# One order for the whole attention-and-mixer kernel, found by list scheduling, in place of a hand-written interleaving

## The chip, the cores and the metric

The kernel runs on one core of a Trainium2 chip. The metric is device time in microseconds (us) of one launch, from DRAM inputs to the DRAM output. The engines are named as in the profile: PE (matrix multiply), PEld (its weight loads), DVE (vector), ACT (scalar), POOL (GpSimd) and SP (here only a queue that issues transfers). Each engine works through its own instructions strictly in the order in which the program emitted them and waits on semaphores where it needs another engine's result.

## The reference, cut to what matters

```python
# q, k, v: 4 batches x 8 heads x 768 x 64; sort_net: 4 x 8 x 8 x 8
P = sort_net
for _ in range(5):                       # 5 Sinkhorn steps on each 8 x 8 matrix
    P = exp(P - max(P, -1)); P = P / (sum(P, -1) + 1e-9); P = P / (sum(P, -2) + 1e-9)
k_sorted, v_sorted = einsum("bhij,bhjcd->bhicd", P, k_blocks), same for v   # 8 blocks of 96 rows
scores = q_b @ k_sorted_b.T / 8          # per block: 96 x 96
x = softmax(scores) @ v_sorted_b         # then heads side by side: x is 4 x 768 x 512
wq, wk = x @ w_q, x @ w_k                # 512 -> 64
mixed = (wq @ wk.T / 8) @ x              # 768 tokens with 768 tokens
out = relu(mixed) @ w_out                # 512 -> 512, float32
```

The maximum that the reference takes off in its softmax cancels, and the kernel leaves it out there. Of the mixer, the kernel forms wk.T @ x (64 x 512) first, and then wq times that.

## The kernel before, in words

Work goes by batch b (4) and block i (8 blocks of 96 tokens). In the text a **unit** is a run of matmuls into one PSUM buffer together with the copy ("eviction") that empties it. The kinds, with the lines of their matmuls and evictions:

- Q (L162; L166 and L167): the queries of two heads, transposed, 12 transposes; two copies into the zero-padded QZ. Four units a batch.
- K (L186; L190): mixes the 8 key blocks by P (through the matrix M) and transposes, 12 matmuls; four units a batch, into KT.
- V (L206; L209): the same for values, 2 matmuls; four units, into VS. Then eight transfers on SP's queue (T, L215) turn VS into VT, one per block.
- S (L228; L235): scores of one block, 4 matmuls; ACT takes the exponential into E. Eight a batch.
- AV (L243; L249 and L250): E times VT with the row sums as a 65th column, 8 matmuls; DVE divides into X. Eight a batch.
- XT (L258; L262): X of two blocks transposed. Four a batch.
- The mixer `moe(b)`: WQ (L270; L275), WK (L281; L284), A (L289; L293), four MIX (L303; L310 on DVE, L312 on ACT) and three OUT units (L320; L326 on ACT, one L324 on DVE), each OUT followed by a transfer of 512 KB to DRAM (L327).

PSUM has three buffers of two banks (`ps`, used by K, V, S, AV, WQ, MIX, OUT) and two of one bank (`ps1`: Q, XT, WK, A). A unit waits until the buffer that it takes in turn has been emptied.

POOL issues the loads: q, k and v of each batch, 768 KB each as they land, in the order Q0 K0 V0 Q1 K1, the three weights, V1 Q2 K2 V2 Q3 K3 V3, with its memsets and the making of M (L173) among them.

What sets the order: the prologue is written out; then a loop goes over the 32 blocks `(b, i)` and emits S one block ahead, AV, and after every second block XT. Between them it emits pieces of a queue `Work`, in equal shares of estimated cost up to block 7: first the Q, K and V units of batch b+1, and from i = 1 on the mixer of batch b-1, strictly one generator after the other. The engine of each eviction is written at the call. The mixer of the last batch runs alone after the loop (`drain(moe(B - 1))`).

Of the kernel before, what the change touches and what calls it, by code (L numbers as in the profile page):

```python
# [17 lines left out]
def kernel(
# [133 lines left out]
    Xb = {}  # L152
    XT = {}
    KT = {}
    VT = {}
    Ms = {}

    def q_unit(b, kp, eng):
# [95 lines left out]
    def xt(b, i0):  # L254
        ps = psum1([P, PT, 2 * BLK], BF16)
        for ii in range(2):
            for pt in range(PT):
# [4 lines left out]
        nc.vector.tensor_copy(XT[b][:, :, i0 * BLK:(i0 + 2) * BLK], ps)  # L262

    def moe(b):
        X, Xt = Xb[b], XT[b]
# [8 lines left out]
        wqT = rot.tile([P, S], BF16, tag="wqT", name="wqT")
        nc.scalar.copy(wqT.rearrange("p (a n) -> p a n", a=2), ps[:, :, 0:hf])  # L275
        yield 8 * 163
        ps = psum1([P, NB, DH])
        for i in range(NB):
            m = P if i < NB - 1 else BLK
            for pt in range(PT):  # L280
                nc.tensor.matmul(ps[0:m, i, :], Xt[:, pt, i * BLK:i * BLK + m], wk_t[:, pt, :],  # L281
                                 start=(pt == 0), stop=(pt == PT - 1), skip_group_check=True)
# [11 lines left out]
        yield 8 * 107
        mixT = rot.tile([P, PT, R6, P], BF16, tag="mixT", name="mixT")
        wqv = wqT.rearrange("p (i r s) -> p r i s", i=NB, r=R6)
        ni = NB // 2
        n = 0
        for p2 in range(2):
            for hh in range(2):  # L300
                ps = psum([P, 2, 512])
                for a in range(2):
                    nc.tensor.matmul(ps[:, a, 0:hf], Ab[a * DH:(a + 1) * DH, p2 * P:(p2 + 1) * P],  # L303
                                     wqv[a * DH:(a + 1) * DH, :, hh * ni:(hh + 1) * ni, :],
                                     start=True, stop=True, skip_group_check=True)
# [151 lines left out]
```

## Time and profile before

| what | value |
|---|---|
| median of 3 runs | 148.35 us (147.12 to 149.61) |
| the profiled execution | 149.07 us; its span, first to last instruction, 147.2 us |
| PE busy | 101.9 us (69%), 1277 matmuls recorded |
| DVE busy | 78.8 us (54%) |
| ACT busy | 72.2 us (49%) |
| mean granted TensorE clock | 0.928 |
| DMA | 19.77 MB, mean 134 GB/s |

How to read it: times are from the span's start. A row of the timeline gives start, length, engine, line, operation and tiles, and in brackets how long the engine stood idle just before and what released it. The length of a group of matmuls contains the last one's run to its end, so the next group can start before it is over. "PEclk" is the share of the full 2.4 GHz that was granted; 0.5 is the lower level, 1.2 GHz.

### The profile page before, as it was taken

What the parts mean: (1) busy time and instruction counts of PE and PEld (TensorE: products, weight loads), DVE (VectorE), ACT (ScalarE), POOL (GpSimd) and SP (SyncE); (2) the same over time, 40 slices, a digit from 0 to 9 for tenths busy, and PEclk for the clock granted to TensorE, in tenths of its full rate; (3) what the DMA queues carried; (4) which work ended last, traced back from release to release, by engine and by line L of the source; (5) the groups of instructions that cost most, each with busy time, mean ns of one, the idle gap of its engine ahead of it and who ended that gap; (6) DMA issues with size and microseconds to landing.
All of it is one profiled execution on the core that took longest, in us unless ns stands there. A gap on an engine that the chain in (4) does not pass through costs nothing.

```text
span 147.2 us, 3040 instructions
## 1 busy us (share of the span) xinstructions
PE 101.9 (69%) x1277; PEld 69.7 (47%) x1284; DVE 78.8 (54%) x171; ACT 72.2 (49%) x97; POOL 28.3 (19%) x31
## 2 busy tenths in 40 slices
PE   0041987349874987778877876788976995965960
PEld 0031946336653946444556473546852454641320
DVE  4876880797777645444489256335464237215030
ACT  4018269444760786636538847355572444213220
POOL 7997499930040000000000000000000000000000
PEclk9999999996999599999999999999997799685599
DMA  1999999999999999903420057035100154000055
GB/s 8 179 204 204 204 205 192 232 246 205 204 204 230 246 205 205 241 11 143 176 109 4 0 97 122 3 159 216 57 0 4 51 215 161 0 4 0 0 222 206
DMA packets 19437, 19.77 MB, mean 134 GB/s; under 512 B 2017, under 2 KB 17889, under 8 KB 19425
## 3 DMA queue, kind: packets, MB, share of 16 engines
q0 software_dynamic: 14064, 10.09, 45.4%
q1 hardware_dynamic: 5360, 9.50, 20.4%
q8 instruction: 10, 0.16, 0.4%
q14 instruction: 3, 0.02, 0.0%
HBM read 20.19 MB, written 6.29 MB: 180 GB/s over the span
## 4 chain that ended last, share of the span: by engine, by line
PE 39%; DVE 17%; DMA 16%; ACT 14%; issue 6%; POOL 6%; ACTq 0%; SPq 0%; DVEq 0%; POOLq 0%
PE ps L320 16%; DMA Vn<-in_v_dram 8%; DMA VT<-VS 7%; ACT ot L326 6%; DVE X L250 5%; DVE mixT L310 4%; PE ps L270 4%; ACT KT L190 4%; PE ps L281 3%; PE ps L243 3%; PE ps L289 3%; PE ps L228 3%; PE ps L258 2%; DVE wkb L284 2%; DVE XT L262 2%
## 5 line engine op out<-in xcount | busy, mean ns | idle before, releaser
L235 ACT ACTIVATE E<-ps 96x768 bf16<-96x768 f32 x32 | 25.3, 808 | 12.0 <-PE ps L228 11.9
L320 PE MATMUL ps<-wo_t,mixT 128*128 128x512 bf16 x89 | 25.8, 429 | 6.3 <-DVE mixT L310 3.7
L326 ACT COPY ot<-ps 128x1024 f32<-128x1024 f32 x11 | 11.1, 1012 | 23.9 <-PE ps L320 17.1
L250 DVE TENSOR_TENSOR X<-ps,R 96x512 bf16<-96x512 f32 x32 | 22.0, 686 | 1.1
L320 PEld LDWEIGHTS <-mixT 128*128 128x128 bf16 x96 | 9.9, 106 | 19.4 <-issue 7.4
L262 DVE COPY XT<-ps 128x768 bf16<-128x768 bf16 x16 | 8.9, 557 | 19.0 <-PE ps L258 18.8
L243 PE MATMUL ps<-VT,E 96*128 96x65 bf16 (+1 forms) x256 | 14.4, 199 | 5.2 <-DMA VT<-VS 3.8
L228 PE MATMUL ps<-QZ,KT 128*96 128x192 bf16 x128 | 15.9, 249 | 2.8 <-ACT E L235 1.7
L243 PEld LDWEIGHTS <-E 96*128 96x128 bf16 (+1 forms) x256 | 12.6, 104 | 8.9 <-issue 4.8
L190 ACT CAST KT<-ps 128x768 bf16<-128x768 f32 x15 | 11.1, 808 | 8.2 <-PE ps L186 8.2
L162 PE MATMUL ps<-idb,Qn 128*64 128x128 bf16 x192 | 8.8, 252 | 8.8 <-DMA Qn<-in_q_dram 8.7
L249 DVE RECIPROCAL R<-ps 96x8 f32<-96x8 f32 x32 | 6.3, 196 | 16.0 <-PE ps L243 16.0
L228 PEld LDWEIGHTS <-KT 128*96 128x96 bf16 x128 | 11.6, 125 | 3.7 <-issue 3.5
L258 PE MATMUL ps<-idb,X 96*128 96x96 bf16 x128 | 9.3, 212 | 5.7 <-DVE X L250 3.6
L162 PEld LDWEIGHTS <-Qn 128*64 128x64 bf16 x192 | 7.3, 130 | 9.7 <-DMA Qn<-in_q_dram 8.7
L258 PEld LDWEIGHTS <-X 96*128 96x128 bf16 x128 | 7.3, 101 | 9.3 <-DVE X L250 4.6
L166 DVE COPY QZ<-ps 64x768 bf16<-64x768 bf16 x14 | 7.7, 547 | 4.9 <-PE ps L162 4.7
L186 PE MATMUL ps<-M,Kn 128*64 128x128 bf16 x192 | 9.5, 270 | 0.7 <-DVE M L173 0.5
L209 ACT CAST VS<-ps 128x768 bf16<-128x768 f32 x11 | 8.5, 813 | 2.3 <-PE ps L206 2.3
L310 DVE TENSOR_SCALAR mixT<-ps 128x768 bf16<-128x768 f32 x8 | 7.5, 954 | 3.8 <-PE ps L303 3.8
L206 PE MATMUL ps<-Vn,M 128*128 128x384 bf16 x32 | 8.5, 377 | 1.2 <-ACT VS L209 0.6
L186 PEld LDWEIGHTS <-Kn 128*64 128x64 bf16 x192 | 8.5, 144 | 1.1 <-issue 1.0
(65 smaller groups left out, 114.7 us busy)
## 6 DMA issues: line engine op xcount, KB each, us to landing
out_dram<-ot SPq DMA_DIRECT2D x12, 512.0 KB, 2.6
VT<-VS SPq DMA_DIRECT2D x32, 97.5 KB, 5.3
Qn<-in_q_dram POOLq DMA_DIRECT2D x4, 768.0 KB, 19.0
Kn<-in_k_dram POOLq DMA_DIRECT2D x4, 768.0 KB, 20.8
Vn<-in_v_dram POOLq DMA_DIRECT2D x4, 768.0 KB, 23.1
wo_t<-in_moe_w_out_dram POOLq DMA_DIRECT2D x1, 512.0 KB, 17.3
wq_t<-in_moe_w_q_dram POOLq DMA_DIRECT2D x1, 64.0 KB, 15.3
wk_t<-in_moe_w_k_dram POOLq DMA_DIRECT2D x1, 64.0 KB, 15.0
```

Of the source, the lines that this page charges most:

```text
L162: nc.tensor.matmul(ps[hh * D:(hh + 1) * D, r, :], Qn[b][:, 2 * kp + hh, r, :], idb, is_transpose=True, start=True, stop=True, skip_group_c ...
L186: nc.tensor.matmul(ps[hh * D:(hh + 1) * D, r * P:(r + 1) * P], Kn[b][:, h, r, :], Ms[b][:, h].rearrange("p i s -> p (i s)"), start=True, s ...
L190: eng(KT[b][:, kp], ps[:, 0:S].rearrange("p (r s) -> p s r", r=R6))
L228: nc.tensor.matmul(ps[0:BLK, kp // 2, (kp % 2) * 2 * BLK:(kp % 2 + 1) * 2 * BLK], KT[b][:, kp, i * SP:(i + 1) * SP].rearrange("p s r -> p ...
L235: nc.scalar.activation(E.rearrange("p (a n) -> p a n", a=2), ps[0:BLK, :, 0:4 * BLK], ACT.Exp, scale=scale)
L243: nc.tensor.matmul(ps[0:m, h // 4, (h % 4) * D1:(h % 4 + 1) * D1], E[:, h * BLK:h * BLK + m], VT[b][:, i, h, :], start=True, stop=True, sk ...
L250: nc.vector.tensor_mul(Xb[b][:, i].rearrange("p (a t d) -> p a t d", a=2, t=4), pv[:, :, :, 0:D], Rt.unsqueeze(3).to_broadcast([BLK, 2, 4, ...
L258: nc.tensor.matmul(ps[:, pt, ii * BLK:(ii + 1) * BLK], Xb[b][:, i0 + ii, pt * P:(pt + 1) * P], idb[0:BLK, 0:BLK], is_transpose=True, start ...
L262: nc.vector.tensor_copy(XT[b][:, :, i0 * BLK:(i0 + 2) * BLK], ps)
L310: nc.vector.tensor_relu(ov, iv)
L320: nc.tensor.matmul(ps[:, rr, :], mixT[:, pt, r0 + rr, :], wo_t[:, pt, :], start=(pt == 0), stop=(pt == PT - 1), skip_group_check=True)
L326: nc.scalar.copy(ot, ps)
```

## The change

The prologue up to M and PTR stays. All later work is described as about 230 objects `Unit` (209 of them planned by the function below, transfers included) with a PE cost, the eviction's cost on each engine allowed, the units it depends on, the units that must have read a buffer before it is overwritten, and a due time from a table `DUE`. `plan` is a list scheduler: among units that its model says could start within 60 ns of the earliest, it takes the one due first, and gives its eviction to the engine that would end it first. The kernel then emits the units in that order. Numbers in the table and in `plan` set the order alone; nothing waits for a time.

Units change too. WQ and WK are two halves each, so that they need only half of XT. MIX is split by token residue rather than by block, so that the first OUT needs only two MIX units. The last batch's OUT is six units of one bank (`ps1`) with transfers of 256 KB. Q, K, V, XT, WQ, WK, A, MIX and OUT may be evicted by ACT or DVE. M has three buffers in place of two, and M of batch 2 is made before the loop. The doubled w_q comes by two loads in place of one load and an ACT copy (L400). Engine, number and size of the other instructions are as before: 2570 rows on PE in both.

```diff
--- before.py
+++ after.py
+SW, LPE, LEV, LSLOT, LDMA = 95, 245, 90, 60, 3500
+SLOTS = {"b": 3, "s": 2}
+FREE = {"PE": 14500, "ACT": 16300, "DVE": 15900, "DMA": 14500}
+LAND = {"Q": [9000, 24500, 35500, 46500], "K": [12500, 28300, 39300, 50300],
+        "V": [16300, 32000, 43000, 54000], "W": 28000}
+PERIOD = 18000
+DUE = {
+    "Q": [(-33441, 1952), (-29592, 640), (-21240, 1562), (-20283, 640)],
...
+}
+class Unit:
+    def __init__(self, key, pe, mode, tag, ev, deps=(), war=(), ready=0):
+        self.key, self.pe, self.mode, self.tag, self.ev = key, pe, mode, tag, ev
+        self.deps, self.war, self.ready = list(deps), list(war), ready
+        off, step = DUE[key[0]][key[1]]
+        self.due = key[1] * PERIOD + off + step * key[2]
+
+def all_units(B, NB, NP, R6):
+    us = []
+
+    def add(*a):
+        us.append(Unit(*a))
+
+    for b in range(B):
+        old = b >= 2
+        kps, hs = range(NP), range(2)
+        s_old = [("S", b - 2, i) for i in range(NB)] if old else []
+        av_old = [("AV", b - 2, i) for i in range(NB)] if old else []
+        mix_old = [("MIX", b - 2, n) for n in range(4)] if old else []
+        outs = [(r, 1) for r in range(R6)] if b == B - 1 else [(r, 2) for r in range(0, R6, 2)]
+        for kp in kps:
+            if b or kp >= 2:
+                add(("Q", b, kp), 320, "c", "s", {"DVE": 1130, "ACT": 1420}, [], s_old,
+                    LAND["Q"][b])
+            add(("K", b, kp), 320, "c", "b", {"ACT": 700, "DVE": 880}, [], s_old, LAND["K"][b])
+            add(("V", b, kp), 326, "f", "b", {"ACT": 700, "DVE": 880}, [], [], LAND["V"][b])
+        qk = [(c, b, kp) for kp in kps for c in "QK" if b or kp >= 2 or c == "K"]
+        for i in range(NB):
+            n = b * NB + i - 8
+            add(("T", b, i), 0, None, None, {"DMA": 600}, [("V", b, kp) for kp in kps], av_old)
+            add(("S", b, i), 332, "f", "b", {"ACT": 700}, qk,
+                [("AV", n // NB, n % NB)] if n >= 0 else [])
+            add(("AV", b, i), 232, "f", "b", {"DVE": 885}, [("S", b, i), ("T", b, i)],
+                [("A", b - 2, 0)] + [("XT", b - 2, j) for j in range(4)] if old else [])
+        for j in range(4):
+            add(("XT", b, j), 344, "f", "s", {"DVE": 474, "ACT": 620},
+                [("AV", b, 2 * j), ("AV", b, 2 * j + 1)],
+                [(c, b - 2, h) for c in ("WK", "WQ") for h in hs] if old else [])
+        for h in hs:
+            xts = [("XT", b, 2 * h), ("XT", b, 2 * h + 1)]
+            add(("WQ", b, h), 652, "f", "b", {"ACT": 420, "DVE": 480}, xts, mix_old, LAND["W"])
+            add(("WK", b, h), 496, "f", "s", {"DVE": 350, "ACT": 370}, xts,
+                [("A", b - 2, 0)] if old else [], LAND["W"])
+        add(("A", b, 0), 856, "c", "s", {"ACT": 330, "DVE": 350},
+            [("WK", b, h) for h in hs] + [("AV", b, i) for i in range(NB)], mix_old)
+        for n in range(4):
+            add(("MIX", b, n), 170, "r", "b", {"ACT": 700, "DVE": 870},
+                [("A", b, 0)] + [("WQ", b, h) for h in hs],
+                [("OUT", b - 2, r) for r in range(0, R6, 2)] if old else [])
+        for r, w in outs:
+            halves = sorted({r * 2 // R6, (r + w - 1) * 2 // R6})
+            add(("OUT", b, r), 864 * w, "f", "b" if w == 2 else "s",
+                {"ACT": 910, "DVE": 1140} if w == 2 else {"ACT": 500, "DVE": 590},
+                [("MIX", b, 2 * h + p) for h in halves for p in range(2)], [], LAND["W"])
+    return us
+
+def plan(us):
+    free = dict(FREE)
+    ring = {t: [0] * n for t, n in SLOTS.items()}
+    pe, ev, order, mode = {}, {}, [], "f"
+    todo = {u.key: u for u in us}
+    while todo:
+        cand = []
+        for u in todo.values():
+            if any(d not in ev for d in u.deps) or any(w not in pe for w in u.war):
+                continue
+            t = max([u.ready] + [ev[d] for d in u.deps])
+            if u.pe:
+                t = max(free["PE"] + (SW if u.mode != mode else 0), t + LEV, ring[u.tag][0] + LSLOT)
+            else:
+                t = max([t, free["DMA"]] + [pe[w] for w in u.war])
+            cand.append((t, u))
+        lim = max(min(t for t, _ in cand), free["PE"]) + 60
+        t, u = min(((t, u) for t, u in cand if t <= lim), key=lambda x: (x[1].due, x[0]))
+        pe[u.key] = t + u.pe
+        src = max([t] + [pe[w] for w in u.war])
+        if u.pe:
+            free["PE"], mode = t + u.pe, u.mode
+            src = max(src, t + u.pe + LPE)
+        eng = min(u.ev, key=lambda e: max(free[e], src) + u.ev[e])
+        free[eng] = max(free[eng], src) + u.ev[eng]
+        ev[u.key] = free[eng] + (LDMA if eng == "DMA" else 0)
+        if u.pe:
+            ring[u.tag] = ring[u.tag][1:] + [free[eng]]
+        del todo[u.key]
+        order.append((u.key, eng, t, free[eng]))
+    return order
...
-    wq_t = const.tile([P, PT, DH], BF16)
+    wqd = const.tile([P, PT, 2, DH], BF16)
...
-    nc.gpsimd.dma_start(out=wq_t, in_=moe_w_q.rearrange("(t p) d -> p t d", p=P))
+    for a in range(2):
+        nc.gpsimd.dma_start(out=wqd[:, :, a, :], in_=moe_w_q.rearrange("(t p) d -> p t d", p=P))
...
-        M = rot.tile([P, H, NB, SP], BF16, tag="M", name="M", bufs=2)
+        M = rot.tile([P, H, NB, SP], BF16, tag="M", name="M", bufs=3)
...
+    def u_WQ(b, h, eng):
+        if b not in wqT:
+            wqT[b] = rot.tile([P, S], BF16, tag="wqT", name="wqT")
         ps = psum([P, 2, 512])
-        for hh in range(2):
+        for pt in range(PT):
+            nc.tensor.matmul(ps[:, 0, 0:hf], wqd[:, pt].rearrange("p a d -> p (a d)"),
+                             XT[b][:, pt, h * hf:(h + 1) * hf],
+                             start=(pt == 0), stop=(pt == PT - 1), skip_group_check=True)
+        copies[eng](wqT[b][:, h * hf:(h + 1) * hf], ps[:, 0, 0:hf])
...
+        rh, p2 = n // 2, n % 2
+        nr = R6 // 2
...
+        w = 1 if b == B - 1 else 2
+        ps = psum([P, 2, 512]) if w == 2 else psum1([P, 1, 512])
...
-    k_unit(0, 0, nc.scalar.copy)
-    k_unit(0, 1, nc.vector.tensor_copy)
-    q_unit(0, 2, nc.vector.tensor_copy)
-    q_unit(0, 3, nc.vector.tensor_copy)
-    k_unit(0, 2, nc.scalar.copy)
-    k_unit(0, 3, nc.scalar.copy)
-    for kp in range(NP):
-        v_unit(0, kp, nc.scalar.copy if kp % 2 else nc.vector.tensor_copy)
-    turn_v(0)
     make_m(1, PTR, nc.gpsimd)
     load_q(3)
     load_k(3)
     load_v(3)
+    make_m(2, PTR, nc.gpsimd)
...
+    emit = {"Q": u_Q, "K": u_K, "V": u_V, "T": u_T, "S": u_S, "AV": u_AV, "XT": u_XT,
+            "WQ": u_WQ, "WK": u_WK, "A": u_A, "MIX": u_MIX, "OUT": u_OUT}
+    for (kind, b, n), eng, _, _ in plan(all_units(B, NB, NP, R6)):
+        if (kind, b, n) == ("S", 1, 0):
+            make_m(3, PTR, nc.gpsimd)
+        emit[kind](b, n, eng)
```

Three places of the order follow; the rows are in emission order, with the program's tile names.

**ACT, around the mixer of batch 0** (`E` the scores of batch 1, `KT` and `VS_87` the preparation of batch 2; `wqT`, `wkb`, `Ab`, `mixT`, `ot` the mixer). Before:

```order
19 L190 CAST KT<-ps 128x768 x4
20 L235 ACTIVATE E<-ps 96x768
21 L209 CAST VS_87<-ps 128x2x6x64 x3
22 L275 CAST wqT<-ps 128x768
23 L235 ACTIVATE E<-ps 96x768
24 L293 ACTIVATE Ab<-ps_942 128x256
25 L312 ACTIVATE mixT<-ps 128x2x6x64
26 L235 ACTIVATE E<-ps 96x768
27 L312 ACTIVATE mixT<-ps 128x2x6x64
28 L326 COPY ot<-ps 128x1024
```

Now:

```order
30 L365 COPY XT<-ps_787 128x4x192
31 L388 CAST wkb<-ps_821 96x256
32 L375 CAST wqT<-ps 128x384
33 L333 ACTIVATE E<-ps 96x768 x2
34 L399 ACTIVATE Ab<-ps_882 128x256
35 L305 CAST KT<-ps 128x768 x2
36 L416 ACTIVATE mixT<-ps 128x2x384 x3
37 L429 COPY ot<-ps 128x1024
38 L333 ACTIVATE E<-ps 96x768
39 L314 CAST VS_87<-ps 128x2x6x64
40 L375 CAST wqT<-ps 128x384
41 L314 CAST VS_87<-ps 128x2x6x64
```

Before, the four K and three V copies stand in one run ahead of the mixer; now two K copies stand between `Ab` and `mixT`, V copies after the first `ot`, and half of batch 1's `wqT` is among them.

**ACT, at the end of the program.** Before:

```order
57 L235 ACTIVATE E<-ps 96x768
58 L326 COPY ot<-ps 128x1024
59 L235 ACTIVATE E<-ps 96x768
60 L275 CAST wqT<-ps 128x768
61 L293 ACTIVATE Ab<-ps_1937 128x256
62 L312 ACTIVATE mixT<-ps 128x2x6x64 x2
63 L326 COPY ot<-ps 128x1024 x2
```

Now:

```order
72 L416 ACTIVATE mixT<-ps 128x2x384 x3
73 L365 COPY XT<-ps_1834 128x4x192
74 L333 ACTIVATE E<-ps 96x768
75 L429 COPY ot<-ps 128x1024 x3
76 L375 CAST wqT<-ps 128x384 x2
77 L399 ACTIVATE Ab<-ps_1952 128x256
78 L416 ACTIVATE mixT<-ps 128x2x384 x2
79 L429 COPY ot<-ps_1988 128x512
```

(Five more rows like the last follow.) Before, one `E` stands behind the last large `ot` of batch 2; now all three `ot` of batch 2 stand behind the last `E`, so that they lie beside the last AV and XT units.

**SP's queue** (`VT<-VS_87` batches 0 and 2, `VT<-VS_88` batches 1 and 3). Before:

```order
1 L65 DMA Pm<-in_sort_net_dram 32x64
2 L215 DMA VT<-VS_87 96x1x520 x8
3 L215 DMA VT<-VS_88 96x1x520 x8
4 L215 DMA VT<-VS_87 96x1x520 x8
5 L327 DMA out_dram<-ot 128x1024 x3
6 L215 DMA VT<-VS_88 96x1x520 x8
7 L327 DMA out_dram<-ot 128x1024 x9
```

Now:

```order
2 L320 DMA VT<-VS_87 96x1x520 x8
3 L320 DMA VT<-VS_88 96x1x520 x8
4 L430 DMA out_dram<-ot 128x1024 x2
5 L320 DMA VT<-VS_87 96x1x520 x6
6 L430 DMA out_dram<-ot 128x1024
7 L320 DMA VT<-VS_87 96x1x520 x2
8 L320 DMA VT<-VS_88 96x1x520 x2
9 L430 DMA out_dram<-ot 128x1024
10 L320 DMA VT<-VS_88 96x1x520 x6
11 L430 DMA out_dram<-ot 128x1024 x5
12 L430 DMA out_dram<-ot 128x512 x6
```

Output transfers, which wait for an `ot`, now stand ahead of parts of the VT transfers of batches 2 and 3.

## Rows read from the trace of the kernel before

**Rows 1.** Stretches of the span: length, busy of each engine, PEclk, DMA.

```profile
0.00:14.50 14.50, 2.12 (x28) 1.76 (x29) 9.87 (x40) 5.62 (x10) 12.62 (x20) 1.00 1.00 148
14.50:51.00 36.50, 26.43 (x428) 21.74 (x428) 25.94 (x50) 19.78 (x28) 15.69 (x11) 0.91 1.31 216
51.00:112.40 61.40, 48.67 (x643) 32.90 (x643) 33.31 (x64) 36.92 (x48) 0.00 (x0) 1.00 0.44 107
112.40:143.50 31.10, 24.67 (x184) 13.29 (x186) 9.67 (x17) 9.87 (x12) 0.00 (x0) 0.78 0.20 78
sum 147.20, PE 101.89 PEld 69.68 DVE 78.80 ACT 72.19 POOL 28.31; mean PE 20.38 PEld 13.94 DVE 15.76 ACT 14.44 POOL 5.66
```

**Rows 2.** The chain that ended last: start, length, what.

```profile
22.74 5.57 DMA VT<-VS
...
41.39 5.22 DMA VT<-VS
...
54.45 1.46 PE ps L270 x8
...
83.23 1.46 PE ps L270 x8
...
142.45 1.01 ACT ot L326
```

**Rows 3.** PE's timeline from 95 to 109 us, at the full clock.

```profile
95.36 1.89 PE L320 MATMUL ps<-wo_t,mixT 128*128 128x512 bf16 x8 [0.19 <-ACT ot L326]
97.08 0.44 PE L243 MATMUL ps<-VT,E 96*128 96x65 bf16 x8
...
100.11 0.51 PE L258 MATMUL ps<-idb,X 96*128 96x96 bf16 x8
100.46 0.43 PE L243 MATMUL ps<-VT,E 96*128 96x65 bf16 x8
...
103.12 0.43 PE L243 MATMUL ps<-VT,E 96*128 96x65 bf16 x8
103.39 0.51 PE L228 MATMUL ps<-QZ,KT 128*96 128x192 bf16 x4
103.73 1.46 PE L270 MATMUL ps<-XT,wqd 128*128 128x384 bf16 x8
105.03 1.16 PE L281 MATMUL ps<-wk_t,XT 128*128 128x64 bf16 x32
106.03 0.44 PE L243 MATMUL ps<-VT,E 96*128 96x65 bf16 x8
...
106.97 1.06 PE L289 MATMUL ps<-X,wkb 96*64 96x256 bf16 x16 [0.16 <-DVE wkb L284]
108.52 0.66 PE L303 MATMUL ps<-wqT,Ab 64*128 64x384 bf16 x6 [0.48 <-ACT Ab L293]
```

**Rows 4.** PE's timeline, other places.

```profile
14.98 1.49 PE L186 MATMUL ps<-M,Kn 128*64 128x128 bf16 x24 [0.52 <-DVE M L173]
...
21.64 0.49 PE L228 MATMUL ps<-QZ,KT 128*96 128x192 bf16 x4
...
28.36 0.44 PE L243 MATMUL ps<-VT,E 96*128 96x65 bf16 x8 [2.27 <-DMA VT<-VS]
28.73 0.86 PE L162 MATMUL ps<-idb,Qn 128*64 128x128 bf16 x24
...
35.25 1.47 PE L206 MATMUL ps<-Vn,M 128*128 128x384 bf16 x4
...
63.98 1.46 PE L320 MATMUL ps<-wo_t,mixT 128*128 128x512 bf16 x6 [0.78 <-DVE mixT L310]
...
112.59 2.77 PE L320 MATMUL ps<-wo_t,mixT 128*128 128x512 bf16 x6 [0.63 <-DVE mixT L310]
```

**Rows 5.** Tile Qn, the one load issued between 12.9 and 13.9 us (batch 2).

```profile
L71 POOL DMA_DIRECT2D Qn<-in_q_dram x1: 893/893/893, 13.0 to 13.0; - x1
...
DMA to landing us min/median/max: 25.7/25.7/25.7
```

More of the change, by code (lines that the diff above doesn't have):

```diff
@@ L149, with u_Q @@
     load_v(2)
[L152 to L158, printed above, removed]
+    Xb, XT, KT, VT, Ms, Es = {}, {}, {}, {}, {}, {}
+    wqT, wkb, Ab, mixT = {}, {}, {}, {}
+    hf = S // 2
+    copies = {"ACT": nc.scalar.copy, "DVE": nc.vector.tensor_copy}
+    def u_Q(b, kp, eng):
         ps = psum1([P, R6, P], BF16)
@@ L273, in moe @@
                                  start=(pt == 0), stop=(pt == PT - 1), skip_group_check=True)
[L274 to L282, printed above, removed]
@@ L294, in moe @@
[L294 to L305, printed above, removed]
-                ov = mixT.rearrange("p (a t) r n -> p a t r n", a=2)[
-                    :, :, p2, :, hh * ni * SP:(hh + 1) * ni * SP]
-                iv = ps[:, :, 0:hf].rearrange("p a (r n) -> p a r n", r=R6)
-                if n % 2:
-                    nc.vector.tensor_relu(ov, iv)
-                else:
-                    nc.scalar.activation(ov, iv, ACT.Relu)
-                n += 1
-                yield 250
@@ L349, in drain, with u_MIX @@
-    def drain(gen):
-        for _ in gen:
-            pass
-    q_unit(0, 0, nc.scalar.copy)
-    q_unit(0, 1, nc.scalar.copy)
+        Ab[b] = rot.tile([P, DM // 2], BF16, tag="Ab", name="Ab")
+        if eng == "ACT":
+            nc.scalar.mul(Ab[b], ps, moe_scale)
+        else:
+            nc.vector.tensor_scalar_mul(Ab[b], ps, moe_scale)
+    def u_MIX(b, n, eng):
+        if b not in mixT:
+            mixT[b] = rot.tile([P, PT, R6, P], BF16, tag="mixT", name="mixT")
+        wqv = wqT[b].rearrange("p (i r s) -> p r i s", i=NB, r=R6)
+        rh, p2 = n // 2, n % 2
+        nr = R6 // 2
+        ps = psum([P, 2, 512])
+        for a in range(2):
+            nc.tensor.matmul(ps[:, a, 0:hf], Ab[b][a * DH:(a + 1) * DH, p2 * P:(p2 + 1) * P],
+                             wqv[a * DH:(a + 1) * DH, rh * nr:(rh + 1) * nr],
+                             start=True, stop=True, skip_group_check=True)
+        ov = mixT[b].rearrange("p (a t) r n -> p a t (r n)", a=2)[:, :, p2, rh * hf:(rh + 1) * hf]
+        if eng == "ACT":
+            nc.scalar.activation(ov, ps[:, :, 0:hf], ACT.Relu)
+        else:
+            nc.vector.tensor_relu(ov, ps[:, :, 0:hf])
@@ new lines, in u_OUT @@
+    def u_OUT(b, r0, eng):
+        od = out[b].rearrange("(p r) e -> p r e", r=R6)
+        w = 1 if b == B - 1 else 2
+        ps = psum([P, 2, 512]) if w == 2 else psum1([P, 1, 512])
+        for rr in range(w):
+            for pt in range(PT):
+                nc.tensor.matmul(ps[:, rr, :], mixT[b][:, pt, r0 + rr, :], wo_t[:, pt, :],
+                                 start=(pt == 0), stop=(pt == PT - 1), skip_group_check=True)
+        ot = rot.tile([P, w, DM], FP32, tag=f"ot{w}", name="ot", bufs=3 if w == 2 else 2)
+        copies[eng](ot, ps)
+        nc.sync.dma_start(out=od[:, r0:r0 + w, :], in_=ot)
@@ L356 @@
+    u_Q(0, 0, "ACT")
+    u_Q(0, 1, "ACT")
     psv = psum([P, NG, NB, NB])
```

154 lines of the change are left out of this document (41 added, 113 removed), and 9 rows, old and new, of the table DUE.

## The prediction

> **What bounds the kernel now.** I read the share of busy time first, then stretches of the span, then the chain of waits, then PE's timeline. No engine is full: after 14.5 us DVE works 68.9 us (78.80 less 9.87) and ACT 66.6 us (72.19 less 5.62) of 132.7 [rows 1]. PE is busy 79% of the stretch from 51.0 to 112.4 us, at the full clock (48.67 of 61.40), and that busy time contains the run-out of the last matmul of each group [rows 1]. The chain returns to the same place every 28.78 us: WQ starts at 54.45 and at 83.23 [rows 2]. So the kernel is a period of one batch, and the question is how much PE work a period holds.
>
> Prices of units at the full clock, start to next start: OUT 1.72 us (95.36 to 97.08), XT 0.35 (100.11 to 100.46), AV 0.27 (103.12 to 103.39), S 0.34, WQ 1.30, WK 1.00 [rows 3]. OUT, WQ and WK all come out 0.16 below their listed length, the run-out. Taking that off: A 1.06 - 0.16 = 0.90; three MIX in 0.66 - 0.16, so 0.17, taken as 0.20 [rows 3]; two Q in 0.86 - 0.16, so 0.35 each [rows 4]. At the low clock six matmuls of OUT take 2.77 us in place of 1.46, a factor of 1.9; two K then take 1.49 and two V 1.47, which gives 0.35 and, rounded down, 0.33 each at the full one [rows 4].
>
> A batch is 4 Q 1.40, 4 K 1.40, 4 V 1.32, 8 S 2.72, 8 AV 2.16, 4 XT 1.40, WQ 1.30, WK 1.00, A 0.90, 4 MIX 0.80, 3 OUT 5.16: 19.56 us, **68% of the period**. Four batches less the two Q of the prologue are 77.5 us. The order before needs from 14.5 to 142.4 us for them [rows 1, 2], a share of 61%. It reaches more only where the preparation of the next batches has ended: from 95.36 to the end of A at 107.87 lie 2 OUT, 5 AV, 5 S, 2 XT, WQ, WK and A, 10.39 us of work in 12.51, **a share of 0.83** [rows 3]. There PE has S, AV and XT to put between the mixer's steps, with the same five PSUM buffers and the same evictions.
>
> **The change, part by part.** *Start.* Up to 14.5 us nothing moves. K, Q and V of batch 0 then stand in another order, but PE works through all ten at the low clock: from 14.98 to 21.64, 6.66 us [rows 4] for 3.42 of work. At a share of 0.83 that would be 4.1, so 2.5 us are added to the sum. The first AV waits for VT, 5.57 us from issue to landing [rows 2]; the last V eviction cannot be earlier than now, so PE's wait of 2.27 us [rows 4] stays. Eight S in place of six stand ahead of it and fill some of that time, but the units behind them were going to be done in any case; it may shrink by a few tenths, and I leave it at 2.3.
>
> *Order.* With units of three batches at hand the list can fill the waits of the mixer's chain: before, PE stands 0.16 us for `wkb` and 0.48 for `Ab` even in its best stretch [rows 3], and 0.78 for `mixT` at 62 to 64 us, when OUT comes next in the queue [rows 4]. What such a list reaches is not in the trace. From below it is bounded by the share of the old period, 0.68; from above by 1. The nearest row is the stretch with most work to choose from, 0.83, and I take that: 77.5 / 0.83 = 93.4 us. The engines that empty PSUM allow it: 135.5 us of evictions on two engines, now free to go to either, are 67.8 each in about 100. The eleven more, smaller copies (4 `wqT`, 4 `wkb`, 3 `ot`) fit beside that: even at 1.01 us, the price of the largest copy [rows 2], they are 11 us on two engines.
>
> *Clock.* Where the first wait for VT ends, the granted clock is 0.91 from 14.5 to 51 us, 3.3 us lost; from 112.4 to 143.5 it is 0.78, 6.8 us lost [rows 1]. Between them, where PE is busy 79%, it is 1.00 throughout. The first wait stays, so I keep half of the early loss, 1.7 us; the late one comes in the mixer of the last batch that stands alone, which now has three OUT units ahead of it and shorter waits, and I take none. The Trainium skill, "TensorE: Matmul & The Clock Gate", section "A second HAM failure mode: psum-queue depth-cycling", speaks against the change: cycling through PSUM buffers makes PE idle briefly between groups, so that the clock falls and recovers again and again. By it the shorter units would bring low stretches all along, and the sum would be that of the second rival, 130, or more. From 51 to 112.4 us the trace does not agree: the same buffers are cycled there, and the clock is 1.00 [rows 1].
>
> *Loads and VT of batch 1.* One more load of w_q puts all later loads back by a few tenths. Q of batch 2 lands at 13.0 + 25.7 = 38.7 [rows 5], about 39 then. In the new order its first unit stands behind 6 Q, 8 K, 8 V, 8 S, 7 AV, 3 XT, half a WK and half a WQ: 14.4 us, or 17.3 at 0.83, so PE comes to it at 14.5 + 2.5 + 2.3 + 1.7 + 17.3 = 38.3. It may wait up to 0.8. VT of batch 1 takes 5.2 us to land [rows 2], and 3.3 us of work lie ahead of its first AV. I take 1.0 for both. M of batch 2 without its old wait, and the ACT copy of w_q that is gone, cost or give nothing: PE waited for neither.
>
> *SP.* Output transfers ahead of VT transfers wait for an `ot`; the VT pieces behind them are for blocks 6 and 7 of batch 2 and blocks 2 to 7 of batch 3, whose AV units stand at least two OUT units later. Priced at zero; without that cover it is one VT landing, 5.2 us.
>
> *End.* The last chain A, MIX, OUT has nothing to cover it: 0.48 for `Ab` [rows 3], and about as much again for the first MIX eviction, 1.1 with rounding. The last copy is 128x512 in place of 1.01 us for 128x1024 [rows 2], about 0.6 with its latency; from the end of the old one, 143.46, to the end of the span are 3.7 us [rows 1, 2], for half the bytes I take 3.2. Together 3.8.
>
> Sum: 14.5 + 2.5 + 2.3 + 1.7 + 1.0 + 93.4 + 1.1 + 3.8 = 120.3 us of span. The profiled execution has 1.9 outside its span, so 122.2, and it is 0.7 above the median: **121.5 us**.
>
> **The rivals.** *The waits come back elsewhere*: a fixed order fits its model, and any event that is late stops PE with work standing behind it. Against it: the table's prices are close to the rows (S 0.332 to 0.34, XT 0.344 to 0.35) [rows 3]. For it: the table has Q of batch 2 land at 35.5 us, and here it lands at 38.7 [rows 5]; a few such errors in a row would do it. At the old period's share of 0.68, 77.5 us take 114.0: 121.5 + 20.6 = 142.
>
> *The clock falls as often as before*: 10.1 us lost in place of 1.7, 121.5 + 8.4 = 130. For it: early on PE is less dense, with VT and loads to wait for.
>
> *Slower*: after the first wait for VT at 28.4 us the clock stays low. By then 6.8 of the 77.5 us are done; 70.7 x 1.9 = 134, and 28.4 + 134 + 3.8 + 1.9 = 168. Low clock fills waits that would be there anyway (16 us), so it makes the kernel slower by 2% (151.3) only from about 45 us of such work on. Against it: after 51 us the clock is back at 1.00 with PE 79% busy, and the new order makes it busier.
>
> *No change*: the order on paper is another, but the share stays at 0.61, because evictions arrive in the same lumps: 148. That the loads take over as the bound I exclude: the DMA share is 1.31 up to 51 us and 0.44 after it [rows 1], and the units of batches 1 and 2 stand ahead of the last ones.
>
> **The numbers.** Forecast case 0.70: the share between 0.75 and 0.90 puts it between 114 and 131. Waits elsewhere 0.08, clock as before 0.14, no change 0.04, slower 0.04. The range of 115 to 131 holds nearly all of the first and most of the clock case. Two per cent, about what a measurement of this kernel can tell from no change, are 145.4 and 151.3: faster 0.92, same 0.04, slower 0.04.
>
> **What would show it.** Right: WQ halves about 23 us apart from batch to batch in the middle; PE over 90% busy there at a clock of 1.00; the first AV still near 28 us; the last OUT group ending near 116. The sum fails if PE waits for VT or a load more than 2 us after the first, if the clock falls after 51 us, or if DVE or ACT, not PE, runs without gaps.

## The result and the profile after

The changed kernel takes **125.14 us** (median of 4 executions, 123.85 to 126.25; a fifth on record beside them took 123.10) against 148.98 (147.12 to 149.75) for the one before on the same chip: a ratio of **0.837 [0.826, 0.849]**. The forecast was 121.5 us, range 115 to 131. The profiled execution took 126.25 us, its span 124.4, its mean granted clock 0.944. Executions of this kernel differ in how long the clock is low: on a second chip six of them ran from 121.98 us at a mean clock of 1.00 to 125.05 at 0.956. So below, executions are compared at like clocks. The ratios, here and in the table of the experiments, leave out executions of either kernel that ran over 1.5% longer than its fastest, so they differ a little from those of the medians.

The page, its busy shares and the row of the granted clock in 40 slices:

```profile
PE 97.2 (78%) x1284; PEld 69.6 (56%) x1284; DVE 72.5 (58%) x160; ACT 83.2 (67%) x118; POOL 29.0 (23%) x32
...
PEclk9999999995557998599999999999999999999999
```

Stretches of the span (length; busy time of PE, PEld, DVE, ACT, POOL; granted clock; DMA share; GB/s), beside [rows 1]:

```profile
14.50:28.50 14.00, 10.77 (x144) 8.06 (x144) 8.58 (x16) 10.60 (x15) 8.44 (x7) 1.00 1.39 206
28.50:52.40 23.90, 21.55 (x317) 17.64 (x318) 15.49 (x31) 16.43 (x24) 8.10 (x6) 0.71 1.28 222
52.40:108.00 55.60, 53.43 (x729) 37.49 (x728) 36.18 (x71) 43.15 (x58) 0.00 (x0) 1.00 0.52 124
108.00:124.40 16.40, 9.37 (x73) 4.69 (x71) 2.34 (x3) 7.38 (x12) 0.00 (x0) 0.99 0.42 160
```

In the middle PE is busy 96% of the time, where it was 79%, and ACT 78% where it was 60%. The list keeps PE supplied there. PE's timeline shows how:

```profile
27.73 0.44 PE L344 MATMUL ps<-VT,E 96*128 96x65 bf16 x8 [1.47 <-DMA VT<-VS]
28.58 0.65 PE L344 MATMUL ps<-VT,E 96*128 96x65 bf16 x8 [0.40 <-DMA VT<-VS]
...
47.06 0.44 PE L344 MATMUL ps<-VT,E 96*128 96x65 bf16 x8 [1.89 <-DMA VT<-VS]
...
74.36 1.06 PE L394 MATMUL ps<-X,wkb 96*64 96x256 bf16 x16
75.25 0.84 PE L301 MATMUL ps<-M,Kn 128*64 128x128 bf16 x24
76.02 0.44 PE L344 MATMUL ps<-VT,E 96*128 96x65 bf16 x8
```

A (L394) is followed at once by two K units of a later batch, an AV and more, while its eviction runs: the wait of 0.48 us before MIX [rows 3] is filled. The waits for VT that remain, 3.8 us in all, end before 48 us. Behind two of them the clock falls. The same columns as above, in shorter stretches:

```profile
25.00:28.50 3.50, 1.70 (x37) 1.30 (x36) 2.48 (x6) 2.27 (x4) 3.43 (x4) 1.00 1.22 231
28.50:31.90 3.40, 3.32 (x50) 2.85 (x51) 2.42 (x5) 1.80 (x3) 3.40 (x3) 0.50 1.23 247
...
35.30:38.80 3.50, 3.50 (x45) 2.63 (x40) 1.65 (x3) 1.96 (x4) 1.30 (x1) 0.50 1.32 203
45.60:49.00 3.40, 1.83 (x44) 1.61 (x45) 1.95 (x5) 1.93 (x3) 0.00 (x0) 1.00 1.23 242
49.00:52.40 3.40, 3.40 (x35) 2.71 (x32) 1.67 (x4) 1.08 (x3) 0.00 (x0) 0.50 1.28 234
```

Before each fall PE has stood waiting for VT and was busy 1.70 us of 3.50 and 1.83 of 3.40; then the clock is at its lower level, 1.2 GHz, though PE is 98 to 100% busy.

At the end there is a wait that nobody named. The chain's first transfer of a last output, and ACT's timeline:

```profile
115.46 2.03 DMA out_dram<-ot
```

```profile
114.85 0.59 ACT L429 COPY ot<-ps 128x512 f32<-128x512 f32 x1 [0.28 <-PE ps L426]
116.75 0.59 ACT L429 COPY ot<-ps 128x512 f32<-128x512 f32 x1 [1.31 <-DMA out_dram<-ot]
...
119.49 0.59 ACT L429 COPY ot<-ps 128x512 f32<-128x512 f32 x1 [1.31 <-DMA out_dram<-ot]
```

Six small OUT copies go through two `ot` buffers of their own, and each buffer is free only when its 256 KB have landed, 2.03 us later. The copies, PE behind them (0.85 us before the last eight matmuls) and the end wait for that.

### The profile page after: what moved, and what is told of

Its sections match the earlier page's. It is cut to its first block, busy times and chain, and to the rows that moved or that the text cites. A ratio compares the mean times of both kernels' runs of the same rounds, so it can differ in the third digit from the quotient of the medians.

```text
span 124.4 us, 3090 instructions
## 1 busy us (share of the span) xinstructions
PE 97.2 (78%) x1284; PEld 69.6 (56%) x1284; DVE 72.5 (58%) x160; ACT 83.2 (67%) x118; POOL 29.0 (23%) x32
## 4 chain that ended last, share of the span: by engine, by line
PE 50%; ACT 15%; DMA 13%; DVE 12%; issue 4%; SPq 2%; POOL 2%; ACTq 0%; DVEq 0%; POOLq 0%
PE ps L426 14%; DMA VT<-VS 10%; PE ps L344 7%; PE ps L326 5%; PE ps L372 4%; ACT mixT L416 4%; PE ps L311 4%; ACT ot L429 3%; PE ps L386 3%; DMA out_dram<-ot 3%; PE ps L394 3%; PE ps L301 3%; ACT VS L314 3%; PE ps L361 3%; ACT E L333 2%
## 5 line engine op out<-in xcount | busy, mean ns | idle before, releaser
L426 PE MATMUL ps<-wo_t,mixT 128*128 128x512 bf16 x96 | 22.5, 379 | 1.0 <-ACT ot L429 0.8
L429 ACT COPY ot<-ps 128x1024 f32<-128x1024 f32 (+1 forms) x15 | 12.6, 842 | 13.0 <-PE ps L426 8.9
L344 PE MATMUL ps<-VT,E 96*128 96x65 bf16 (+1 forms) x256 | 15.2, 206 | 5.0 <-DMA VT<-VS 3.8
L344 PEld LDWEIGHTS <-E 96*128 96x128 bf16 (+1 forms) x256 | 12.9, 108 | 8.2 <-DMA VT<-VS 4.5
L426 PEld LDWEIGHTS <-mixT 128*128 128x128 bf16 x96 | 9.1, 98 | 10.6 <-issue 1.8
L350 DVE RECIPROCAL R<-ps 96x8 f32<-96x8 f32 x32 | 6.4, 200 | 12.9 <-PE ps L344 12.6
L416 ACT ACTIVATE mixT<-ps 128x768 bf16<-128x768 f32 x11 | 8.3, 810 | 0.8 <-PE ps L411 0.7
L305 ACT CAST KT<-ps 128x768 bf16<-128x768 f32 x10 | 7.8, 802 | 0.9 <-PE ps L301 0.9
L314 DVE CAST VS<-ps 128x768 bf16<-128x768 f32 x6 | 5.7, 961 | 4.5 <-PE ps L311 4.5
L311 PE MATMUL ps<-Vn,M 128*128 128x384 bf16 x32 | 7.8, 357 | 0.5 <-DVE KT L305 0.2
L301 PEld LDWEIGHTS <-Kn 128*64 128x64 bf16 x192 | 7.6, 133 | 0.5 <-issue 0.3
L365 DVE COPY XT<-ps 128x768 bf16<-128x768 bf16 x9 | 5.0, 551 | 5.0 <-PE ps L361 4.9
```

The source lines that it names most:

```text
L301: nc.tensor.matmul(ps[hh * D:(hh + 1) * D, r * P:(r + 1) * P], Kn[b][:, h, r, :], Ms[b][:, h].rearrange("p i s -> p (i s)"), start=True, s ...
L311: nc.tensor.matmul(ps[:, hh, 0:R6 * D], Ms[b][:, h].rearrange("p i s -> p (i s)"), Vn[b][:, h].rearrange("p r d -> p (r d)"), start=True, ...
L314: copies[eng](VS[b % 2][:, :, 2 * kp:2 * kp + 2, 0:D].rearrange("p r h d -> p h r d"), ps[:, :, 0:R6 * D].rearrange("p h (r d) -> p h r d" ...
L344: nc.tensor.matmul(ps[0:m, h // 4, (h % 4) * D1:(h % 4 + 1) * D1], E[:, h * BLK:h * BLK + m], VT[b][:, i, h, :], start=True, stop=True, sk ...
L416: nc.scalar.activation(ov, ps[:, :, 0:hf], ACT.Relu)
L426: nc.tensor.matmul(ps[:, rr, :], mixT[b][:, pt, r0 + rr, :], wo_t[:, pt, :], start=(pt == 0), stop=(pt == PT - 1), skip_group_check=True)
```

## The experiments

| run | what | median us (range) | clocks | ratio to before |
|---|---|---|---|---|
| e1 | new units, old order, old engines | 142.52 (140.47 to 144.94) | 0.921 to 0.967 | 0.976 [0.952, 1.001] |
| e2 | new order, old units, old engines | 129.48 (127.58 to 129.53) | 0.952 to 0.968 | none given |
| e3 | new order, new units, old engines | 128.50 (128.18 to 128.82) | 0.954 to 0.974 | 0.888 [0.883, 0.893] |
| e4 | the changed kernel again | 123.66 (121.98 to 125.05) | 0.953 to 1.000 | 0.836 [0.828, 0.844] |
| e5 | six halves of `ot` at the end | 121.30 (119.76 to 122.71) | 0.958 to 0.995 | 0.817 [0.810, 0.824] |
| e6 | unused matmuls in the VT waits | 122.12 (122.09 to 122.25) | 0.988 to 1.000 | 0.832 [0.828, 0.837] |
| e7 | M of batch 1 early, table replanned | 125.50 (123.69 to 126.55) | 0.961 to 0.991 | 0.849 [0.840, 0.858] |
| e8 | e5 and e6 together | 120.19 (120.13 to 120.44) | 0.991 to 1.000 | 0.828 [0.824, 0.832] |
| e9 | due times searched anew, M early, six halves | **116.66** (116.35 to 117.48) | 0.978 to 1.000 | 0.804 [0.799, 0.809] |
| e10 | M of batch 1 early, old table | 124.43 (123.23 to 125.92) | 0.945 to 0.980 | 0.864 [0.851, 0.876] |

e1 to e3 ran on one chip, e4 to e9 on a second, e10 on a third. e4 was expected at 124 to 126 us and came a little lower at the median; its low stretches follow the same two waits for VT as those of the first profile.

### Which part of the change gave the gain: e1, e2, e3

**e1** keeps the new units and writes them out in the old interleaving:

```diff
-    for (kind, b, n), eng, _, _ in plan(all_units(B, NB, NP, R6)):
+    for (kind, b, n), eng in old_order(all_units(B, NB, NP, R6), B, NB, NP, R6):
```

> The changed units (WQ, WK in halves, MIX by residue, last OUT in six small units, M with three buffers, w_q by two loads), emitted in the interleaving and with the eviction engines of the kernel before. If the order does the work: the chain preparation, WQ, WK, A, MIX, OUT stands as before, one after the other, and only the mixer's tail gets shorter by the first OUT that needs two MIX: 142 to 149 us, PE busy about 79% from 51 to 112 us as before. If the smaller units do the work: 133 us or less, PE busy over 90% in the middle.

**e2** keeps the list and undoes the units (whole WQ and WK, MIX by blocks, three wide OUT in the last batch) and the free choice of engine:

```diff
-        kps, hs = range(NP), range(2)
+        kps, hs = range(NP), range(1)
...
-            add(("WQ", b, h), 652, "f", "b", {"ACT": 420, "DVE": 480}, xts, mix_old, LAND["W"])
+            add(("WQ", b, h), 1304, "f", "b", {"ACT": 700}, xts, mix_old, LAND["W"])
```

> List scheduling with the units and the eviction engines of the kernel before (WQ and WK whole, MIX by block, OUT always two banks). If the order does the work: WQ, WK and MIX fill the waits of other batches although they are larger: 125 to 134 us. If the smaller units do the work: 138 us or more, with PE waiting for wkb, Ab and mixT as in the kernel before. The due times were set for halves, so a few us over the changed kernel are no sign of either.

**e3** keeps list and units, and gives each eviction the engine that it had before:

```diff
-            add(("XT", b, j), 344, "f", "s", {"DVE": 474, "ACT": 620},
+            add(("XT", b, j), 344, "f", "s", {"DVE": 474},
```

> The changed units and list scheduling, but every eviction on the engine of the kernel before (XT, Q, WK on DVE, K, V, WQ, A, OUT on ACT, MIX by turns); 7 XT and 5 Q copies that ACT has in the changed kernel go back to DVE, 6 K and 6 V copies back to ACT, and the order is planned anew for that. If the choice of engine matters: waits of PE for an eviction come back, 129 to 133 us. If the order alone matters: within 2 us of the 125.1 of the changed kernel.

The order theory holds. At a clock of 0.944 the units alone are worth 2 to 3 us (142.1 and 142.9 against 144.8 for before on the same chip), and the ratio's interval, 0.952 to 1.001, leaves open whether that is anything; one execution of e1 (140.47) lies below the forecast range, and PE is busy 84% from 51 to 112 us (51.25 of 61.0) where 79% was expected. The order alone is worth 15 to 17 us at like clocks (127.6 and 129.5 at 0.952 to 0.954 against 144.6 at 0.958) and 18 at the medians of the same chip (129.5 against 147.3). All three variants keep the third buffer of M and the two loads of w_q. Units on top of the order without free engines show no gain clear of the spread (127.6 and 129.5 us for e2, 128.2 and 128.8 for e3, at 0.952 to 0.955).

With the free choice of engine comes a step that the forecast put at nothing: at 0.953 to 0.956, 128.2 to 128.8 us for e3 and 124.3 to 125.1 for the changed kernel in e4, about 4 us, on two chips. The middle stretch of e1, of e3 and of e4 shows both steps:

```profile
52.40:108.00 55.60, 46.94 (x620) 31.76 (x620) 30.57 (x63) 34.49 (x49) 0.00 (x0) 1.00 0.47 114
```

```profile
52.40:108.00 55.60, 49.98 (x669) 34.96 (x667) 37.13 (x76) 37.70 (x51) 0.00 (x0) 1.00 0.49 114
```

```profile
52.40:108.00 55.60, 53.44 (x714) 36.93 (x710) 35.71 (x70) 42.83 (x58) 0.00 (x0) 1.00 0.53 133
```

PE goes from 46.94 to 49.98 to 53.44 us of 55.60. In the last step DVE works 1.4 us less and ACT 5.1 us more; neither was full before. By the profile's list of waits PE stands about 4 us for copies of ACT there in e3, 0.7 us for DVE and 0.3 for VT, and about 1.5 us for ACT alone in e4: waits for an eviction came back, as expected, though the time lies just under the 129 to 133 us. That an eviction which may go to the engine that is free empties its PSUM buffer sooner is how I read it. Not shown is how much of the 4 us is the choice itself: e3 was planned anew and has another order (it puts V of batch 1 ahead of K, and PE stands 2.51 us before it, at 35.22), and its due times, like those of e2, were not searched for fixed engines; e9 shows that a search can be worth several us.

### The tail: e5

```diff
-        ot = rot.tile([P, w, DM], FP32, tag=f"ot{w}", name="ot", bufs=3 if w == 2 else 2)
+        if r0 % 2 == 0:
+            ots[b] = rot.tile([P, 2, DM], FP32, tag="ot", name="ot", bufs=3)
+        ot = ots[b][:, r0 % 2:r0 % 2 + w, :]
```

> The six last OUT copies of the program write the six halves of the three wide ot tiles in place of two ot1 tiles in turn, so that no copy waits for an output transfer (waits of 1.31 and 1.31 us on ACT in the changed kernel's last chain, 0.85 us on PE). Theory A, the two buffers cost what the waits show: 1.5 to 2.5 us less than the changed kernel on the same chip (span about 122). Theory B, the transfers themselves are the limit (a 256 KB output takes 2.0 us to land, and six of them follow one another): within 0.5 us of the changed kernel, the last transfers landing no earlier.

ACT's last copies no longer wait for a transfer:

```profile
111.28 0.59 ACT L431 COPY ot<-ps 128x512 f32<-128x512 f32 x1 [0.34 <-PE ps L426]
112.10 0.59 ACT L431 COPY ot<-ps 128x512 f32<-128x512 f32 x1 [0.23 <-PE ps L426]
...
113.84 0.59 ACT L431 COPY ot<-ps 128x512 f32<-128x512 f32 x1 [0.23 <-PE ps L426]
```

At a clock of 0.994 to 1.00 it takes 119.8 to 120.0 us against 121.98: 2.0 us, theory A. The pair e6 and e8, whose executions all kept their clock, gives the same edit 1.9 us (122.12 and 120.19).

### The clock: e6, e8

```diff
+        if (kind, b, n) in (("AV", 0, 0), ("AV", 1, 0)):
+            ps = psum1([P, 512])
+            for _ in range(8):
+                nc.tensor.matmul(ps, idb, QZ[0][:, 0, 0, 0:512], start=True, stop=True,
+                                 skip_group_check=True)
         emit[kind](b, n, eng)
```

> Eight extra matmuls of 128x512 (0.21 us each at full clock, 1.7 us) whose result is not used, put ahead of the first AV of batch 0 and again ahead of the first AV of batch 1, where PE waits 1.47 and 1.89 us for VT in the changed kernel. Theory A, the low clock from 28.5 to 38.8 and 49.0 to 52.4 us follows from PE's idle time just before: the granted clock stays at 1.00 after 28.5 us, and the time falls by 3 to 6 us. Theory B, it follows from the many small matmuls of 65 and 96 columns in those stretches, on which PE is 97 to 100% busy: the clock is as low as before, and the time is the same or up to 1 us longer. Theory C, the low clock hides behind loads and VT anyway: the clock rises but the time moves by less than 1 us, with new waits for DMA between 30 and 50 us.

All six executions ran at 0.988 to 1.000 within 0.16 us of each other. The same stretches as of after:

```profile
14.50:28.50 14.00, 11.71 (x147) 8.35 (x148) 8.32 (x14) 10.58 (x15) 8.41 (x7) 1.00 1.39 206
28.50:52.40 23.90, 22.07 (x423) 17.78 (x421) 18.16 (x38) 19.80 (x29) 8.11 (x6) 1.00 1.28 222
31.90:35.30 3.40, 2.69 (x66) 2.26 (x63) 2.41 (x6) 3.35 (x6) 3.40 (x4) 1.00 1.31 211
```

Theory A has the mechanism and not the size: the clock stays up when the two waits are filled with work, but the time falls by 1.5 us at the medians, and by 2.2 to 3.0 against the executions of e4 at 0.953 to 0.956, where 3 to 6 were expected. Theory B falls, since the small matmuls are all still there. The one execution of the changed kernel that kept its clock in e4 took 121.98, about as long as e6, so by it the matmuls cost next to nothing. How much the low clock costs is best read from where A of batch 0 starts on PE, because behind it four runs of this order are alike: from there to WK of the last batch PE takes 55.1 us in each.

| run | A of batch 0, us | last WK, us | low clock before |
|---|---|---|---|
| after | 52.82 | 107.94 | 28.5 to 38.8, 49.0 to 52.4 |
| e4 | 50.86 | 105.97 | most of 28.5 to 35.3, part of 45.6 to 52.4 |
| e5 | 48.33 | 103.44 | none |
| e6 | 48.69 | 103.80 | none |

So it cost about 4.5 us in the first profile (52.82 - 48.33; 0.6 of it are longer waits for VT, 3.8 against 3.2) and 2.5 in e4's. That is less than the 6.5 us that 13.7 us at the lower level would be worth (13.7 x (1 - 1/1.9)): at the full clock PE has gaps there instead. From 31.9 to 35.3 us it is busy 2.69 of 3.40 us in e6 and waits for ACT's copies into QZ and KT (0.41 and 0.30 us); ACT is full, 3.35.

The waits allow a low clock and do not force it: e5 has nearly the same waits (1.27, 0.45, 1.16 and 0.31 us for VT), and three of its six executions ran at 0.994 to 0.995. The Trainium skill, "TensorE: Matmul & The Clock Gate", section "HAM oscillation — how this bites in real kernels", has a wait for a transfer as what lowers the clock. The rows of after from 25.0 to 31.9 us and those of e6 agree, with shorter waits than the page's case; the executions of e5 at 0.994 show that such a wait is not enough by itself, and e7 below has falls without one. Why the clock then stays low until 38.8 us with PE 98 to 100% busy, no run settles.

> Both edits of the last runs together: the last OUT copies in six halves of the wide tiles, and eight unused matmuls ahead of the first AV of batches 0 and 1. If the clock explains the spread of single executions (119.8 to 120.0 us at a clock of 0.994 and 122.6 us at 0.958 with the six halves alone; 122.1 us in all six with the matmuls alone) the two add: 119.8 to 120.3 us in every execution, clock over 0.985. If the matmuls only shift which executions fall, single executions of 122 us and more remain.

The two edits add: 120.1 to 120.4 in every execution, two of the six 0.1 above the expected range.

### Filling the waits with real work: e7, e10, e9

**e7** moves M of batch 1 ahead on POOL and gives the planner the landing times that the trace of after shows:

```diff
-SW, LPE, LEV, LSLOT, LDMA = 95, 245, 90, 60, 3500
+SW, LPE, LEV, LSLOT, LDMA = 95, 245, 90, 60, 5500
-LAND = {"Q": [9000, 24500, 35500, 46500], "K": [12500, 28300, 39300, 50300],
-        "V": [16300, 32000, 43000, 54000], "W": 28000}
+LAND = {"Q": [9000, 20500, 39200, 53400], "K": [12500, 25100, 43000, 57300],
+        "V": [16300, 35300, 48400, 61100], "W": 30000}
...
     make_m(1, PTR, nc.gpsimd)
+    load_k(2)
...
+    load_v(2)
```

> M of batch 1 is computed on POOL ahead of the issues of the K and V loads of batch 2 and the QZ and VS memsets of the second buffers (they start at 21.7 us and M of batch 1 only at 28.25 us in the changed kernel), and the planner's table has the landing times and the VT delay (5.5 us for 3.5) that the changed kernel's trace shows. Theory A, the waits for VT are there because nothing else was ready: K of batch 1 (4 units of 0.35 us) and more fill the wait at 26.3 us, the waits for VT fall from 3.8 us to under 1.5 us, and the time falls by 2 to 3 us, by 5 or more if the clock then also stays at 1.00. Theory B, POOL is held by the loads' issues ahead of M (waits of 2.82 and 3.35 us at 16.6 and 20.8 us), so M starts hardly earlier, or what fills the waits is missing later: within 1 us of the changed kernel.

M starts at 17.23 us in place of 28.25, and no wait of PE for VT of 0.2 us or more is left. Yet the kernel is slower: 123.69 us at 0.991 against 121.98 at 1.000, of which about 0.5 us belongs to the clock (e4 takes 1.0 us longer at 0.980), and 125.50 against 123.66 at the medians. The stretch 52.4 to 108 us tells where:

```profile
52.40:108.00 55.60, 51.56 (x662) 35.34 (x662) 34.01 (x68) 39.06 (x53) 0.00 (x0) 0.97 0.52 129
```

PE is busy 51.56 us of it where it was 53.44 in e4. It waits there 2.4 us for copies of ACT and 1.4 for DVE, where e4 has 1.5 for ACT alone. That what was done early is missing later fits this and is not shown further. Neither theory had it right: A's waits went, and the loss is over B's 1 us. The clock of 0.97 is a fall in the middle of the kernel, with no transfer waited for:

```profile
72.90:76.30 3.40, 2.37 (x52) 1.82 (x49) 3.01 (x9) 1.73 (x3) 0.00 (x0) 1.00 0.60 135
76.30:79.70 3.40, 3.40 (x39) 2.22 (x36) 2.36 (x4) 2.14 (x4) 0.00 (x0) 0.52 0.00 0
```

```profile
74.45 0.34 PE L356 MATMUL ps<-idb,X 96*128 96x96 bf16 x4 [0.31 <-DVE X L346]
...
75.37 0.34 PE L406 MATMUL ps<-wqT,Ab 64*128 64x384 bf16 x2 [0.31 <-DVE R L345]
76.12 0.45 PE L339 MATMUL ps<-VT,E 96*128 96x65 bf16 x8 [0.41 <-DVE X L346]
```

Short waits for DVE, 0.3 to 0.4 us each, stand ahead of it; at 31.9 us the clock falls behind the like (0.52 to 35.3 us). So a wait for a transfer is not needed either. **e10** makes the POOL edit alone, with the changed kernel's table.

> M of batch 1 ahead on POOL as in the run with M early, but the planner's table as in the changed kernel, so that PE, ACT and DVE have the changed kernel's order. If the loss of that run (123.7 us at a clock of 0.99 where the changed kernel takes 122.0) came from the order that the new table gave: 122.0 us where the clock is over 0.99, the waits for VT as in the changed kernel. If it came from POOL (the K load of batch 2 and what follows it issued at another time, the memsets of the second QZ later): 123.5 us or more at such a clock.

At like clocks it equals the changed kernel: 123.23 at 0.980 (e4: 123.0 at 0.980), 124.2 to 124.5 at 0.953 to 0.954 (e4: 124.3 and 124.7). None of its executions had a clock over 0.99, so the expected 122.0 itself was not seen. The loss of e7 therefore goes with the order that the truer table gave, not with POOL: with the landing times corrected and the due times left as they were, the list is worse.

**e9** therefore searches the due times anew on the corrected model, with M early and the six halves (one row of the table; the landing of Q of batch 1 stands in it at 24.2 us, where the trace of after gives 20.5):

```diff
-    "K": [(-12000, 1000), (-5894, 800), (6869, 262), (-3508, 1562)],
+    "K": [(-12794, 430), (-5919, 716), (15161, 918), (-8149, 1562)],
```

> Another order: the table of due times was searched anew with the landing times and VT delay of the changed kernel's trace, M of batch 1 goes ahead on POOL (with the memsets of the second QZ behind it), and the last OUT copies have six halves. Theory A, the changed kernel's order is not yet what PE allows: from 14.5 us to the last chain PE of the run with six halves was idle for about 9.5 us in all (3.3 to 28.5 us, 3.3 to 52.4 us, 2.9 behind); an order that takes half of it gives about 115 us, range 113.5 to 117.5. Theory B, as in the run with M early, what fills the waits for VT is missing later and the end comes no earlier: 119.5 to 122 us. If the clock falls in some executions, they are up to 3 us longer in either.

```profile
14.50:28.50 14.00, 12.89 (x202) 10.35 (x204) 8.93 (x15) 11.65 (x17) 11.89 (x10) 1.00 1.39 203
28.50:52.40 23.90, 20.50 (x361) 16.55 (x357) 20.02 (x41) 20.27 (x30) 4.42 (x3) 1.00 1.28 223
52.40:108.00 55.60, 52.60 (x683) 36.03 (x689) 32.91 (x66) 41.96 (x59) 0.00 (x0) 1.00 0.56 138
```

PE works 12.89 us of the first 14 behind the prologue (10.77 in after), the clock stays at 0.978 to 1.000 without unused matmuls, and two OUT units of the third batch are left to stand among the six of the last, so that no wait interrupts the end:

```profile
102.09 8.82 PE L421 MATMUL ps<-wo_t,mixT 128*128 128x512 bf16 x39
```

116.66 us, theory A: 3.5 us below e8, 7.0 below the changed kernel in e4. It is the fastest version run, and beats both kernels. How much of it the early M gives beside the new order was not tried by itself; with the old table (e10) it gives nothing.

## Why the prediction was right, step by step

The total was right, 121.5 against 121.98 us where the clock held and 125.14 at the median of the first chip; the mechanism, an order that fills the waits of the mixer's chain with units of other batches, is what e2 shows. That the number came so close is in part luck: two terms were too small (5.6 us up to 52.82 us, 1.2 at the end), one too large (2.6, the share), and the 121.98 us belong to an execution without the low clock, for which the sum had 1.7. Its terms, against the profiled execution, whose span is 4.1 us over the forecast's 120.3:

- *The share.* From A of batch 0 at 52.82 to WK of the last batch at 107.94 us lie 47.9 us of work at the forecast's prices (77.5 less 21.0 before and 8.7 after) in 55.1: **0.87**, where 0.83 was taken, 2.6 us less. The nearest rows [rows 3] were close; e3, whose middle stretch is less busy, points for the excess at the free choice of engine, which the forecast used only to say that the evictions fit.
- *Start.* Right in size: K, Q and V of batch 0 took 6.2 us (14.42 to 20.65), for 4.1 + 2.5. But not all ten ran at the low clock, as the forecast read it: the first five are long, and from 18.79 us a unit has its length at the full clock (a V unit 0.48 us, as at 60.88). (The clock column gives 1.00 for 14.5 to 18.0 us, so only the lengths show it.) The rest are waits for copies of KT and VS.

```profile
14.42 1.49 PE L277 MATMUL ps<-idb,Qn 128*64 128x128 bf16 x24
...
18.79 0.48 PE L311 MATMUL ps<-Vn,M 128*128 128x384 bf16 x2 [0.17 <-ACT KT L305]
```

- *Up to 52.82.* 21.0 us of work took 38.4; the forecast gives 21.0 / 0.83 and 2.5 + 2.3 + 1.7 + 1.0, 32.8. Here lies the miss of **5.6 us**, and it has two halves. The term of the low clock was 1.7 and measured about 4.5 in this execution, by the table of A above: 2.8 us too small. At the full clock (e5) the stretch still takes 33.9 us (48.33 - 14.42), against 31.1 without that term: another 2.8. The waits for VT are no part of these (3.2 us in e5, 2.3 + 1.0 in the sum); it is the share, since 0.83 comes from a stretch without loads to wait for, and here they are late and ACT is full in places. That was not tried by itself; e9, where PE works 12.89 of the first 14 us, shows that some of the time was not forced.
- *The second wait for VT.* 5.2 us to land was taken [rows 2]; it took 6.25, and PE stood 1.89 us:

```profile
22.50 6.04 DMA VT<-VS
...
42.08 6.25 DMA VT<-VS
```

- *SP's queue at zero.* Right: PE waits for VT nowhere after 48 us.
- *The end.* From 107.94 on, 8.66 / 0.83 + 1.1 + 3.8 = 15.3 were forecast, 16.5 measured. The smaller copies were counted as a gain and the buffers behind them not: 2.0 us by e5, so the other terms of the end were 0.8 too large together. The late low clock, taken as gone, is gone.
- *What would show it.* First WQ halves of batch 0 to 3 start at 39.88, 61.30, 86.67 and 108.46, 22.9 us apart on the mean, for 23; PE 96% busy at 1.00, for over 90; the first AV at 27.7, for 28; the last OUT group ends at 119.3, for 116, later by the low clock and the wait for `ot`. One sign of failing was met, by little: PE waits for VT 2.29 us after the first wait (0.40 + 1.89), over the 2 us.
- *The rivals.* "Waits elsewhere" did not come for this table, but e7 shows that it can, with a table only slightly different. "The clock falls as often as before" came in half, early and not late. The rule on depth-cycling named with it (the Trainium skill, "TensorE: Matmul & The Clock Gate", section "A second HAM failure mode: psum-queue depth-cycling") is not borne out in this kernel: from 52.4 to 108 us more, shorter units cycle through the same buffers at 1.00. In e7 the clock does fall there, at 76.3 us behind short waits for copies.

## What to carry to other kernels

Price a reordering by the busiest stretch that the old trace shows, where PE has the most kinds of work to choose from, and treat start and end apart; here that came within 4 us of the median. An eviction that may go to either engine seems to be worth time even where neither engine is full. Where output copies are made smaller, count their buffers against the landing time of a transfer, and where a planner's figures are corrected, search its priorities again.

## What was not expected of the hardware

- The same program keeps its clock in some executions and not in others: e5 ran at 0.994 to 0.995 three times and at 0.958 three times, 119.8 to 120.0 and 122.6 to 122.7 us. Sixteen matmuls whose result nobody uses, in time that was idle anyway, took that spread away (e8).
- The clock also fell where PE waited for copies only, 0.3 to 0.4 us at a time (e7, 0.52 from 76.3 to 79.7 us).
- A 256 KB output takes 2.03 us to land, over twice the 0.87 us that PE needs for the unit that fills it (3.63 us for four units at 112.92, less the run-out), so two buffers are too few although the transfers overlap.
